# A written-out step order, eight plain products and accumulating transfers in the third stage and MLP of a spectral block

## The chip, the cores and the metric

The kernel runs on one core of a Trainium2 chip, in one launch. The metric is the device time of an execution in microseconds, as the median of several executions. The engines are TensorE (PE in the profile, with its weight loads as PEld), VectorE (DVE), ScalarE (ACT), GpSimd (POOL) and SyncE (SP). Each works off its own queue in order; they meet in semaphores. Transfers are issued from SP, ACT or GpSimd queues.

## The reference

```python
mod = (silu(c) @ w_mod).reshape(1, 6, 1, 512)
sa, ca, ga, sb, cb, gb = ...                # six vectors of 512
h = layernorm(x) * (1 + ca) + sa            # x: 2048 positions x 512
X = rfft2(h) * (w_r + 1j * w_i)
x = x + ga * irfft2(X, s=(2048, 512))
h = layernorm(x) * (1 + cb) + sb
h = h @ w1 + b1                             # 512 -> 1376
act = h * tanh(softplus(h))                 # Mish
x = x + gb * (act @ w2)                     # 1376 -> 512
```

All inputs and outputs are 32-bit floats.

## The kernel before, in words

`x` stays in on-chip memory as sixteen tiles `x[:, n, :]` of 128 positions by 512. The transforms are matrix products. The first stage takes rows and part of the columns forward, the second multiplies by the weights, and the third goes back: `p3_col(n)` does columns (16 short PE records at L744 and L745), ScalarE copies the result, `p3_row(n)` does rows (8 at L754) and VectorE adds them to `x` at L757. `norm_sums`, `norm_scale` and `norm_one` make the second layernorm of a tile; `transpose_in` and `scale_in` turn it so that features lie on partitions.

The MLP works on four pairs `i` of position blocks; a block `b` has 256 positions. The inputs of a pair are four quarters `B11`, `B21`, `B12`, `B22` (halves of the 512 features by block). The 1376 hidden features come in groups `t`: `t` = 1 to 5 have 256 each, `t` = 0 has the last 96. Matrix products use a reduced 32-bit format, so every operand is split in a high and a low part: ScalarE rounds to the high part, another engine subtracts for the low one (`split`, L791 and L792; `split_in`, L735 and L736; `split_w1`, L690 and L692), and three products (`TERMS`) are added for each.

For `t` > 0 both matrix products are made in seven products for eight, with sums of operand quarters. Going up, `up(i, t, j)` (L845) is product `j` of six matmuls of 256 columns; its operands are sums of w1 quarters (`sum_w1`, GpSimd at L686) and sums of inputs (`sum_in`, GpSimd at L731). `evict` takes the results out of the banks by ScalarE (L850, L868) and by additions on VectorE (L862, L866, L873); Mish is applied on ScalarE. The seven w1 operands of each `t` are written to DRAM once (`keep_w1`) and fetched for later pairs (`fetch_w1`, eight buffers `wr`).

Going down, `sums(b, t)` builds four 128-column sums on VectorE (L910), `halves` splits them into `ah` and `al`, and `down(b, t, c)` (L940, L936) is one of seven pieces of three matmuls; the w2 sums come from `sum_w2` (GpSimd at L788). After the last group `gather` copies two banks, `chain` adds on VectorE (L970 to L978), and `residual` applies the gate `gb` and adds to `x`, on GpSimd at L984 to L990. `store` writes two tiles of `x` to the output from SP. For the last block, `t` = 3, 4, 5 and 0 go down plainly with w2 rows that are already multiplied by the gate (`gate_w2`, GpSimd at L811), and `finish` adds and stores piece by piece.

The order of the work is that of a list: `plan.at(key, fn, ...)` notes a step with a number, `plan.run()` sorts by it and calls the steps, and each call appends its instructions to the queues of the engines. There are two such lists: one for the third stage with the weights' first preparation, and one for the MLP. In the first list, `plan_w1` prepares w1 groups 2, 3 and 1. In the second, every product has a place in `units`, and the others' keys are counted from these places.

Of the kernel before, what the change touches and what calls it, by code (L numbers as in the profile page):

```python
# [12 lines left out]
P = 128  # L13
# [6 lines left out]
NT = 6  # L20
# [8 lines left out]
FL = F - (NF - 1) * P  # L29
LAST = ((0, 0, D), (1, 0, D // 2), (1, D // 2, D))  # L30
POOL_LOW = range(1, 15, 2)


@with_exitstack
def tile_spectral_block(ctx: ExitStack, tc: tile.TileContext, x_d, w1_d, b1_d, w2_d,
# [615 lines left out]
    slots = {b: pm.tile([P, 2, 2, 256], F32R, name=f"h{b}", tag=f"h{b}") for b in ("B11", "B21", "T1", "T2", "T3", "T4")}  # L651
    wsum = pm.tile([P, 512], F32, name="wsum")
    ring, raws, src = {}, {}, {}
    near = ((1, "A11"), (2, "A11"), (1, "A12"), (1, "S2"), (1, "S1"), (1, "S3"), (2, "A12"), (1, "A22"))
# [4 lines left out]
    def load_w1(t, at, halves=range(2)):  # L659
        for i in halves:  # L660
            r = odd[at + i]
            nc.sync.dma_start(r.rearrange("p (k f) -> p k f", k=2), w1v[:, 2 * i:2 * i + 2, 256 * t - 256:256 * t])
            for j in range(2):
                src[t, f"A{j + 1}{i + 1}"] = r.rearrange("p (k f) -> p k f", k=2)[:, :, P * j:P * j + P]

    def space(t, a, k):
        if (t, a) in ring:
            return
        w = act.tile([P, 7, P], F32R, name=("ah", "al")[k % 2]).rearrange("p e s -> p (e s)")
        ring[t, a] = w[:, 0:512].rearrange("p (i k f) -> p i k f", i=2, k=2)  # L670
# [8 lines left out]
    def sum_w1(t, a):  # L679
        p, q, op = {"S1": ("A21", "A22", ALU.add), "S2": ("S1", "A11", ALU.subtract),  # L680
                    "S3": ("A11", "A21", ALU.subtract), "S4": ("A12", "S2", ALU.subtract)}[a]
        k = ("S1", "S2", "S4", "S3").index(a)
        if (t, a) in ((2, "S4"), (4, "S4"), (5, "S3")):
            src["S"] = even[2] if t < 4 else flat2(kiv) if t == 4 else buf("h")
        src[t, a] = (wsum if k < 2 else src["S"])[:, 256 * (k % 2):256 * (k % 2) + 256].rearrange("p (k f) -> p k f", k=2)
        nc.gpsimd.tensor_tensor(src[t, a], src[t, p], src[t, q], op=op)  # L686

    def split_w1(t, a):
        w = ring[t, a]
        nc.scalar.copy(w[:, 0], src[t, a])  # L690
        eng = nc.vector if a[0] == "A" else nc.gpsimd
        eng.tensor_tensor(w[:, 1], src[t, a], plain(w[:, 0]), op=ALU.subtract)  # L692

    def keep_w1(t, a):
        w = ring[t, a] if t > 3 or t == 1 and (t, a) in near else ring.pop((t, a))
        nc.sync.dma_start(kept[t, a], plain(w.rearrange("p i k f -> p (i k f)")))

    def single_w1(load):
        if load:
            src[0] = buf("g2")[:, 0:4 * FL].rearrange("p (k f) -> p k f", k=4)  # L700
            nc.sync.dma_start(src[0], w1v[:, :, (NF - 1) * P:F])
            return
        nc.scalar.copy(w1s[:, 0], src[0])
        nc.gpsimd.tensor_tensor(w1s[:, 1], src[0], plain(w1s[:, 0]), op=ALU.subtract)
# [22 lines left out]
    def sum_in(b, dst=None):  # L727
        p, q = {"T1": ("B12", "B11"), "T2": ("B22", "T1"), "T3": ("B22", "B12"), "T4": ("B21", "T2")}[b]
        p, q = raws[p], raws[q]
        raws[b] = raws[dst] if dst in raws else dst if dst is not None else buf("h")  # L730
        nc.gpsimd.tensor_tensor(raws[b], p, q, op=ALU.subtract)  # L731

    def split_in(b):
        r = raws[b]
        nc.scalar.copy(part(b, 0), r)  # L735
        nc.vector.tensor_tensor(part(b, 1), r, plain(part(b, 0)), op=ALU.subtract)  # L736
# [100 lines left out]

    def up(i, t, j):
        a, b = PRODUCTS[j]
        w, h = ring.pop((t, a)), slots[b]  # L840
        o = region(i, t, j)
        n = 0
        for p, q in TERMS:
            for k in range(2):
                nc.tensor.matmul(o, w[:, p, k, :], h[:, q, k, :], start=(j in (1, 5) and n == 0), stop=(n == 5),  # L845
                                 skip_group_check=True)
                n += 1

# [118 lines left out]
    def chain(b):  # L967
# [5 lines left out]
        if b == NB - 1:  # L973
            nc.vector.tensor_tensor(r0[:, 0:256], out_ps[b][2][:, 0:256], q[:, 256:], op=ALU.add)
            nc.gpsimd.tensor_tensor(r0[:, 256:], q[:, 256:], p[:, 256:], op=ALU.add)
# [5 lines left out]
    def residual(b):  # L981
        p, q = done.pop(b)
        r0, r1 = rows(b)
        nc.gpsimd.tensor_tensor(r1[:, 256:], r1[:, 256:], q[:, 0:256], op=ALU.add)  # L984
        if b < NB - 1:
            nc.gpsimd.tensor_tensor(r0[:, 256:], r0[:, 256:], p[:, 256:], op=ALU.add)
        for i, r in enumerate((r0, r1)):
            xb = x[:, 2 * b + i, :]
            nc.gpsimd.tensor_tensor(r, r, gbr, op=ALU.mult)
            nc.gpsimd.tensor_tensor(xb, xb, r, op=ALU.add)  # L990
# [16 lines left out]
    class Plan(list):  # L1007
# [7 lines left out]
    def plan_w1(plan, t, load, key, step, at):  # L1015
        k = 7 * (t - 2)
        plan.at(load, load_w1, t, at)
        for i, a in enumerate(("A11", "S1", "A12", "S2", "A22", "S4", "S3")):
            now = key + step * i
            plan.at(now, space, t, a, k + i)  # L1020
            if a[0] == "S":
                plan.at(now + 0.01, sum_w1, t, a)
            late = now + 0.02 if a[0] == "A" else now + 3.4 * step
            plan.at(late, split_w1, t, a)
            plan.at(late + 0.55 * step, keep_w1, t, a)

    plan = Plan()
    for s in range(N2 + 1):
        if s < N2:
            plan.at(s, p3_col, s)  # L1030
        if s:
            plan.at(s + 0.1, p3_row, s - 1)
            plan.at(s + 0.3, norm_sums, s - 1)
# [7 lines left out]
    for k, s in enumerate((0, 0, 1, 2, 3)):  # L1041
        plan.at(s + 0.05, late_mod, k)
    plan.at(5.08, plus_one, cols[:, 1, 1, :], cols[:, 1, 1, :])
    for lo, hi, s in ((0, 2, 4), (2, 4, 7), (4, 8, 13), (8, 12, 15)):
        plan.at(s + 0.2, norm_scale, lo, hi)
    for t, *at in ((1, 0, 2, 2, 3, 5), (2, 4, 8, 6, 7, 9), (3, 9, 11, 11, 12, 14)):
        for s, fn, *args in zip(at, (load_w2, split_w2, sum_w2, sum_w2, split_w2), (t,) * 5,
                                (None, False, 0, 2, True), (None, None, 1, 3, None)):
            plan.at(s + 0.6, fn, *[a for a in args if a is not None])
    plan.at(13.6, load_w2, 0)  # L1050
    plan.at(8.5, w2_space, 2)
    plan.at(16.5, w2_space, 4)
    plan.at(1.8, single_w1, True)
    plan.at(5.4, single_w1, False)
    plan_w1(plan, 2, 0.7, 2.1, 0.5, 0)
    plan_w1(plan, 3, 2.5, 5.7, 0.5, 2)
    for t, a in near:
        if t == 1:
            plan.at(9, slot_w1, (t, a))
        else:  # L1060
            plan.at(9, fetch_w1, t, a)
    plan_w1(plan, 1, 6.5, 9.3, 0.5, 0)
    plan.at(12, load_w1, 4, 2)
    first_raw = {}

    def first_in(b, n, g):
        first_raw[b] = buf("g2") if b in ("B11", "B21") else even[1 if b == "B12" else 0]
        transpose_in(n, g)
        scale_in(b, g, first_raw[b])

    for n, s in ((0, 5), (1, 6), (2, 8), (3, 9)):
        plan.at(s + 0.7, norm_one, n)
    for b, n, g, s in (("B11", 0, 0, 7), ("B21", 0, 1, 8), ("B12", 2, 0, 10), ("B22", 2, 1, 11)):
        plan.at(s + 0.55, first_in, b, n, g)
    for b, s, dst in (("T1", 12, "B11"), ("T2", 12, None), ("T3", 13, None), ("T4", 13, "B21")):
        plan.at(s + 0.5, sum_in, b, dst)
    for b, s in (("B11", 11), ("B21", 12), ("T2", 14), ("T1", 14.5), ("T3", 15), ("T4", 16)):
        plan.at(s + 0.4, split_in, b)
    plan.run()

    cr = big.tile([P, 2, 2, 2, 256], F32R, name="hcr", tag="cr")
    slots["B12"], slots["B22"] = cr[:, 0], cr[:, 1]
    odd[:] = [buf("g1"), buf("g1")] + odd
    turn = turns([even[2], odd[3], even[1], even[0], scb], [even[2], even[1], even[0], scb]), turns([], odd)

    units = [(0, 1, 1), (0, 2, 1), (0, 1, 2), (0, 1, 6), (0, 1, 5), (0, 1, 7), (0, 2, 2), (0, 1, 4), (0, 1, 3),
             (0, 2, 6), (0, 2, 5), (0, 2, 7)]
    for i in range(NB // 2):
        for t in range(1 if i else 3, NT):
            if t == NT - 1:  # L1090
                units += [(i, 0, u) for u in range(4)]
            prev = (i, t - 1) if t > 1 else (i - 1, NT - 1)
            units += [(i, t, 1)] + [prev + (j,) for j in (4, 3)] + [(i, t, j) for j in (6, 2, 5, 7)]
    units += [(NB // 2 - 1, NT - 1, j) for j in (4, 3)]
    where = {u: k for k, u in enumerate(units)}

    plan = Plan()
    for k, (i, t, j) in enumerate(units):
# [5 lines left out]
        plan.at(k, up, i, t, j)  # L1104
        plan.at(k + 0.05, evict, i, t, j)
        if j == 3:
            plan.at(k + 1.5, mish_odd, i, t)
        a = PRODUCTS[j][0]
        if i == 0 and t > 3:
            plan.at(k - 7.9, slot_w1, (t, a))  # L1110
            plan.at(k - (7.5 if t == 4 else 4.7), split_w1, t, a)
            plan.at(k - 3, keep_w1, t, a)
        elif k >= 8:
            plan.at(k - 7.9, fetch_w1, t, a)
    DOWN = (1, 2, 3, 0, 4, 5)
    start = {}
    key = where[0, 0, 0] + 0.25
    for b in range(NB):
        for t in DOWN if b < NB - 1 else (1, 2, 3, 4, 5, 0):
            if b == 0:  # L1120
                key = 0.25 + dict(zip(DOWN, (11, 18, 25, 32, 36, 42)))[t]
# [19 lines left out]
        plan.at(at + 1.6, residual, b)  # L1141
# [213 lines left out]
```

## Time and profile before

| | |
|---|---|
| median of 3 executions | 441.46 us (441.35 to 441.88) |
| the profiled execution | 443.01 us |
| its span, first to last instruction | 441.0 us |
| mean granted TensorE clock | 0.949 |
| busy: PE, DVE, ACT, POOL | 392.6, 333.1, 255.9, 203.1 us |

The span is the time between the first and the last instruction that the profile shows. A group's row gives line, engine, operation, out<-in tiles with shapes, count, then busy microseconds, mean nanoseconds of one, and idle time of the engine before it with what ended it. In a row of waits stand the waiting engine and what it was to write, the one waited for, microseconds in total, times, and the longest. In a row of a time window stand its bounds and length, busy time and count for each engine, the granted clock, and the transfers' share and rate. In a timeline row stand start and duration in microseconds; pieces of the chain of work that ended last have the same two numbers in front.

### The profile page before, as it was taken

The page shows a single profiled execution, that of the slowest core. Times are in us where ns is not written, and L with a number is a line of the kernel's source. Part 1 is how long each engine was busy: PE and PEld are TensorE (multiplying, and loading weights), DVE is VectorE, ACT ScalarE, POOL GpSimd, SP SyncE. Part 2 cuts the span into 40 slices and gives each one's busy share as a digit, 9 for nine tenths or more (in the row PEclk, how much of TensorE's full clock was granted, in tenths as well). Part 3 has the DMA queues.
Part 4 walks back from the last instruction along what each step waited for, and adds up shares of the span by engine and source line. Part 5 has one row for each costly group of instructions (what it writes and reads, how often), then busy time and mean ns, then how long its engine had stood idle before and what let it go on. Part 6 is the DMA issues. An engine that isn't in the chain of part 4 may idle for free.

```text
span 441.0 us, 8229 instructions
## 1 busy us (share of the span) xinstructions
PE 392.6 (89%) x2886; PEld 368.3 (84%) x2886; DVE 333.1 (76%) x659; ACT 255.9 (58%) x560; POOL 203.1 (46%) x227
## 2 busy tenths in 40 slices
PE   9999999999897667996979998979998979999576
PEld 8899777799897667986869998969998969998465
DVE  2999778869899676646783599783599894599984
ACT  2888799845784268853627746526746623535430
POOL 0687488826779034273050075050075060086554
PEclk9999999999998878996989999988999999999969
DMA  8999987766583667174636526535527546624011
GB/s 265 366 350 329 358 287 241 239 210 216 187 281 111 207 214 217 47 255 150 191 107 203 169 76 211 171 107 184 167 89 217 158 115 205 187 78 138 24 49 48
DMA packets 45593, 81.87 MB, mean 186 GB/s; under 512 B 6992, under 2 KB 12208, under 8 KB 45296
## 3 DMA queue, kind: packets, MB, share of 16 engines
q1 hardware_dynamic: 43392, 74.39, 52.3%
q10 hardware_dynamic: 2160, 6.95, 5.0%
q8 instruction: 23, 0.38, 0.4%
q14 instruction: 18, 0.15, 0.1%
HBM read 67.95 MB, written 13.37 MB: 184 GB/s over the span
## 4 chain that ended last, share of the span: by engine, by line
PE 50%; DVE 33%; ACT 7%; DMA 4%; issue 4%; POOL 1%; SPq 1%; DVEq 0%; ACTq 0%; POOLq 0%
PE bank L845 14%; PE bank L940 11%; DVE buf L910 10%; DVE al L792 7%; PE bank L500 3%; PE bank L210 3%; PE bank L549 2%; PE bank L255 2%; DVE w2a L792 2%; PE bank L480 2%; DVE hB L736 2%; DMA w_S<-al 2%; DVE st L124 1%; ACT ah L791 1%; PE bank L952 1%
## 5 line engine op out<-in xcount | busy, mean ns | idle before, releaser
L845 PE MATMUL bank<-hT,wr 128*128 128x256 f32 x480 | 76.3, 299 | 15.5 <-DVE even L862 8.7
L845 PEld LDWEIGHTS bank<-hT,wr 128*128 128x128 f32 x480 | 67.8, 206 | 17.2 <-DVE even L862 9.5
L984 POOL TENSOR_TENSOR modr<-modr,buf 128x256 f32<-128x256 f32 x7 | 6.6, 942 | 126.9 <-DVE buf L971 126.9
L791 ACT CAST ah<-buf 128x512 fp32r<-128x512 f32 (+1 forms) x45 | 27.0, 603 | 42.0 <-DVE buf L910 38.4
L792 DVE TENSOR_TENSOR al<-buf,ah 128x512 fp32r<-128x512 f32 (+1 forms) x45 | 42.8, 957 | 8.9 <-ACT ah L791 8.5
L845 PE MATMUL bank<-hB,wr 128*128 128x256 f32 x240 | 40.8, 313 | 1.8 <-ACT odd L850 1.7
L940 PE MATMUL bank<-w2a,ah 128*128 128x256 f32 x161 | 39.5, 309 | 0.0
L845 PEld LDWEIGHTS bank<-hB,wr 128*128 128x128 f32 x240 | 35.6, 216 | 3.6 <-ACT odd L850 2.9
L940 PE MATMUL bank<-w2b,ah 128*128 128x256 f32 x147 | 33.8, 291 | 0.0
L940 PEld LDWEIGHTS bank<-w2a,ah 128*128 128x128 f32 x161 | 30.5, 219 | 0.0
L940 PE MATMUL bank<-w2a,al 128*128 128x256 f32 x56 | 18.8, 336 | 10.8 <-DVE al L792 10.8
L850 ACT ACTIVATE odd<-bank,b1n 128x256 f32<-128x256 f32 x25 | 11.8, 474 | 27.4 <-PE bank L845 27.3
L940 PEld LDWEIGHTS bank<-w2b,ah 128*128 128x128 f32 x147 | 25.6, 199 | 0.0
L744 PE MATMUL bank<-kc,d 128*128 128x128 f32 x128 | 24.8, 276 | 0.5 <-ACT d L393 0.5
L745 PE MATMUL bank<-kc,d 128*128 128x128 f32 x128 | 24.8, 275 | 0.0
L940 PE MATMUL bank<-w,ah 128*128 128x256 f32 x112 | 22.9, 296 | 0.6 <-DVE modr L978 0.5
L940 PEld LDWEIGHTS bank<-w2a,al 128*128 128x128 f32 x56 | 12.9, 231 | 12.6 <-DVE al L792 12.6
L731 POOL TENSOR_TENSOR buf<-buf 128x512 f32<-128x512 f32 x13 | 18.2, 1411 | 9.5 <-DVE hB L736 8.1
L124 DVE BATCH_NORM_STATS2 st<-x 128x6 f32<-128x512 f32 x32 | 22.0, 688 | 0.3
L990 POOL TENSOR_TENSOR x<-x,modr 128x512 f32<-128x512 f32 x14 | 21.0, 1501 | 1.1
L754 PE MATMUL bank<-kiv,buf 128*128 128x128 f32 x128 | 18.1, 287 | 3.5 <-DVE x L757 2.7
L255 PE MATMUL bank<-buf,mring 128*128 128x512 f32 x48 | 20.6, 430 | 0.2 <-DVE buf L248 0.2
(308 smaller groups left out, 1261.4 us busy)
## 6 DMA issues: line engine op xcount, KB each, us to landing
wr<-w_S SPq DMA_DIRECT2D x69, 256.0 KB, 2.8
wr<-w_A SPq DMA_DIRECT2D x51, 256.0 KB, 2.8
x<-in_A_x_dram SPq DMA_DIRECT2D x16, 256.0 KB, 5.1
xring<-in_x_t_dram SPq DMA_DIRECT2D x16, 256.0 KB, 5.1
out_dram<-x SPq DMA_DIRECT2D x7, 512.0 KB, 4.0
buf<-in_B_w_dram SPq DMA_DIRECT2D x12, 256.0 KB, 3.9
w_S<-wr SPq DMA_DIRECT2D x11, 256.0 KB, 3.0
odd<-in_B_w_dram SPq DMA_DIRECT2D x10, 256.0 KB, 3.4
```

The lines of the kernel that those rows point to most:

```text
L124: nc.vector.bn_stats(t, x[:, n, :])
L255: nc.tensor.matmul(pa, m[:, a, 0:128], g, start=(i == 0), stop=False)
L731: nc.gpsimd.tensor_tensor(raws[b], p, q, op=ALU.subtract)
L744: nc.tensor.matmul(o, dj[:, 0:128], kc[0][:, n, :], start=True, stop=False)
L745: nc.tensor.matmul(o, dj[:, 64:192], kc[1][:, n, :], start=False, stop=True)
L754: nc.tensor.matmul(px[:, j * P:(j + 1) * P], e[:, j * P:(j + 1) * P], kiv[:, j, :], start=True, stop=True)
L791: nc.scalar.copy(h, r)
L792: nc.vector.tensor_tensor(l, r, plain(h), op=ALU.subtract)
L845: nc.tensor.matmul(o, w[:, p, k, :], h[:, q, k, :], start=(j in (1, 5) and n == 0), stop=(n == 5), skip_group_check=True)
L910: nc.vector.tensor_tensor(o, p, q, op=op)
L940: nc.tensor.matmul(out_ps[b][n][:, 256 * half:256 * half + 256], a[p][:, e], w2[t][q][:, r], start=(t == 1 and half == 0 and i == 0), stop ...
L990: nc.gpsimd.tensor_tensor(xb, xb, r, op=ALU.add)
```

## The change

The third stage and the MLP become one list of 1155 steps. Its keys are sorted as before, and then the steps are called in the order that the string `ORDER` writes out by place in the sorted list.

The first pair of blocks (512 positions) is computed with eight plain products for `t` = 1 to 5: each quarter of the result is accumulated in a bank and evicted by one Mish activation on ScalarE (`plain_evict`). Its w1 quarters are split into the buffers from which `up` reads them (`block_w1`), three of the four are kept for later pairs.

The four sums of w1 quarters, which only later pairs read, are built in place by transfers from DRAM that add to their destination, issued from the GpSimd queue (`sum_w1`, steps 0 and 1); step 2 splits a sum and writes it out. The residual of blocks 0 to 6 is multiplied by the gate in one VectorE instruction of 1024 columns and added to `x` by such a transfer. All other arithmetic that GpSimd did in these stages goes to VectorE.

```diff
--- before.py
+++ after.py
...
+PLAIN = {(0, t) for t in range(1, NT)}
...
+ORDER = (
+    "3-4 71 0-1 16 21 2 15 14 5-7 73 38 47 8 12 9 62 13 10 69 86 17 24 84 52 19 79 11 26 126 95 18 22 32 23 87 27 "
...
+    def load_w1(t):
+        src[t] = shared("T1" if t % 2 else "T2").rearrange("p (k f) -> p k f", k=4)
+        nc.sync.dma_start(src[t], w1v[:, :, 256 * t - 256:256 * t])
 
...
+    def split_w1(w, r):
+        nc.scalar.copy(w[:, 0], r)
+        nc.vector.tensor_tensor(w[:, 1], r, plain(w[:, 0]), op=ALU.subtract)
+
+    def block_w1(t, a):
+        slot_w1((t, a))
+        split_w1(ring[t, a], w1_block(t, a, src[t]))
+
+    def keep_w1(t, a, w=None):
+        w = ring[t, a] if w is None else w
         nc.sync.dma_start(kept[t, a], plain(w.rearrange("p i k f -> p (i k f)")))
+
+    def sum_w1(t, a, step):
+        if not temps:
+            temps[0] = shared("T4").rearrange("p (n k f) -> p n k f", n=4, k=2)
+            temps[1] = wsum.rearrange("p (n k f) -> p n k f", n=2, k=2)
+            stage[0] = shared("T3", F32R).rearrange("p (n i k f) -> p n i k f", n=2, i=2, k=2)
+        v = temps[1][:, a == "S3"] if t % 3 == 0 else temps[0][:, 2 * (t % 3 - 1) + (a == "S3")]
+        if step == 0:
+            if a == "S3":
+                nc.scalar.mul(v, w1_block(t, "A21", src[t]), -1.0)
+            if a == "S2":
+                nc.scalar.mul(v, v, -1.0)
+            if a == "S1":
+                nc.sync.dma_start(v, w1_block(t, "A21"))
+                return
+        if step < 2:
+            nc.gpsimd.dma_start(v, w1_block(t, {"S1": "A22", "S2": "A11", "S3": "A11", "S4": "A12"}[a]), accum_op=ALU.add)
+            return
+        n = stage[1] = stage.get(1, 0) + 1
+        w = stage[0][:, n % 2]
+        split_w1(w, v)
+        keep_w1(t, a, w)
 
...
-        p, q = {"T1": ("B12", "B11"), "T2": ("B22", "T1"), "T3": ("B22", "B12"), "T4": ("B21", "T2")}[b]
+        p, q, op = {"T1": ("B12", "B11", ALU.subtract), "T2": ("T1", "B22", ALU.subtract),
+                    "T3": ("B22", "B12", ALU.subtract), "T4": ("B21", "T2", ALU.add)}[b]
         p, q = raws[p], raws[q]
         raws[b] = raws[dst] if dst in raws else dst if dst is not None else buf("h")
-        nc.gpsimd.tensor_tensor(raws[b], p, q, op=ALU.subtract)
+        nc.vector.tensor_tensor(raws[b], p, q, op=op)
...
-            nc.gpsimd.tensor_tensor(tsum[:, o], a, b, op=ALU.subtract)
+            nc.vector.tensor_tensor(tsum[:, o], a, b, op=ALU.subtract)
...
-            nc.gpsimd.tensor_tensor(r, r, gbr[:r.shape[0]], op=ALU.mult)
+            nc.vector.tensor_tensor(r, r, gbr[:r.shape[0]], op=ALU.mult)
...
+    def plain_place(t, f, e):
+        return (e, f) if t == 1 else (f, e)
+
     def up(i, t, j):
-        a, b = PRODUCTS[j]
-        w, h = ring.pop((t, a)), slots[b]
-        o = region(i, t, j)
+        a, b = j if (i, t) in PLAIN else PRODUCTS[j]
+        w, h = ring[t, a], slots[b]
+        if (i, t) in PLAIN:
+            at, half = plain_place(t, int(a[1]) - 1, int(b[2]) - 1)
+            if (i, t, at) not in ups:
+                ups[i, t, at] = bank("AD"[at])
+            o = ups[i, t, at][:, 256 * half:256 * half + 256]
+            first, last = a[2] == "1" and half == 0, a[2] == "2"
+        else:
+            o = region(i, t, j)
+            first, last = j in (1, 5), True
         n = 0
         for p, q in TERMS:
             for k in range(2):
-                nc.tensor.matmul(o, w[:, p, k, :], h[:, q, k, :], start=(j in (1, 5) and n == 0), stop=(n == 5),
+                nc.tensor.matmul(o, w[:, p, k, :], h[:, q, k, :], start=(first and n == 0), stop=(last and n == 5),
                                  skip_group_check=True)
                 n += 1
+
+    def plain_evict(i, t, f, e):
+        b = 2 * i + e
+        if (b, t) not in raw:
+            hold(b, t)
+        at, half = plain_place(t, f, e)
+        nc.scalar.activation(raw[b, t][:, 256 * f:256 * f + 256], ups[i, t, at][:, 256 * half:256 * half + 256], AF.Mish,
+                             bias=b1n[:, 2 * t - 2 + f:2 * t - 1 + f])
 
...
-    def residual(b):
-        p, q = done.pop(b)
+    def residual(b, step):
+        p, q = done[b]
         r0, r1 = rows(b)
-        nc.gpsimd.tensor_tensor(r1[:, 256:], r1[:, 256:], q[:, 0:256], op=ALU.add)
+        if step == 0:
+            nc.vector.tensor_tensor(r1[:, 256:], r1[:, 256:], q[:, 0:256], op=ALU.add)
+            if b < NB - 1:
+                nc.vector.tensor_tensor(r0[:, 256:], r0[:, 256:], p[:, 256:], op=ALU.add)
+            return
         if b < NB - 1:
-            nc.gpsimd.tensor_tensor(r0[:, 256:], r0[:, 256:], p[:, 256:], op=ALU.add)
+            r = modr[:, 0:2]
+            nc.vector.tensor_tensor(r, r, gbr.unsqueeze(1).to_broadcast([P, 2, D]), op=ALU.mult)
+            nc.gpsimd.dma_start(x[:, 2 * b:2 * b + 2, :], r, accum_op=ALU.add)
+            return
         for i, r in enumerate((r0, r1)):
             xb = x[:, 2 * b + i, :]
-            nc.gpsimd.tensor_tensor(r, r, gbr, op=ALU.mult)
-            nc.gpsimd.tensor_tensor(xb, xb, r, op=ALU.add)
+            nc.vector.tensor_tensor(r, r, gbr, op=ALU.mult)
+            nc.vector.tensor_tensor(xb, xb, r, op=ALU.add)
 
...
-            for _, _, fn, args in sorted(self, key=lambda e: e[:2]):
+            steps = [e[2:] for e in sorted(self, key=lambda e: e[:2])]
+            places = [[int(n) for n in run.split("-")] for run in ORDER.split()]
+            places = [k for run in places for k in range(run[0], run[-1] + 1)]
+            assert sorted(places) == list(range(len(steps)))
+            for k in places:
+                fn, args = steps[k]
                 fn(*args)
...
+    S_KEYS = ((1, -5, 1 / 3), (2, 4, 1.7), (3, 11, 1.5), (4, 18, 1.4), (5, 26, 1.1))
     plan = Plan()
...
+    for n in range(N2):
+        last = n == N2 - 1
+        plan.at(n - N2, p3_col, n)
+        plan.at(1.5 if last else n - N2 + 1.1, p3_row, n)
+        plan.at(1.6 if last else n - N2 + 1.3, norm_sums, n)
 
...
+    for t, key in ((1, -15.3), (2, -13.5), (3, -3.9), (4, 5), (5, 12.6)):
+        plan.at(key, load_w1, t)
...
+    for t, key, scale in S_KEYS:
+        for a, step, at in (("S1", 0, 0), ("S3", 0, 0.5), ("S1", 1, 2.2), ("S3", 2, 4), ("S1", 2, 5.5), ("S2", 0, 5.9),
+                            ("S2", 2, 9), ("S4", 1, 9.6), ("S4", 2, 12.6)):
+            plan.at(key + scale * at, sum_w1, t, a, step)
+
...
             plan.at(k, up_single, i, j)
@@ -1102,23 +1206,23 @@
                 plan.at(k + 0.05, evict_single, i)
             continue
         plan.at(k, up, i, t, j)
+        if (i, t) in PLAIN:
+            f, e = int(j[0][1]) - 1, int(j[1][2]) - 1
+            at, half = plain_place(t, f, e)
+            if j[0][2] == "2" and half:
+                for h in range(2):
+                    plan.at(k + 0.05, plain_evict, i, t, *((h, e) if t == 1 else (f, h)))
+            continue
         plan.at(k + 0.05, evict, i, t, j)
         if j == 3:
             plan.at(k + 1.5, mish_odd, i, t)
...
+        plan.at(k - 7.9, fetch_w1, t, PRODUCTS[j][0])
...
-        plan.at(at + 1.6, residual, b)
+        plan.at(at + 1.6, residual, b, 0)
+        plan.at(at + 2.6, residual, b, 1)
         plan.at(at + 9, store, b)
...
```

More of the change, by code (lines that the diff above doesn't have):

```diff
@@ L1079, in tile_spectral_block, with late_slots @@
[L1079 to L1087, printed above, removed]
+        plan.at(s - N2 + 0.55, first_in, b, n, g)
+    def late_slots():
+        cr = big.tile([P, 2, 2, 2, 256], F32R, name="hcr", tag="cr")
+        slots["B12"], slots["B22"] = cr[:, 0], cr[:, 1]
```

197 lines of the change are left out of this document (78 added, 119 removed), and 43 rows, old and new, of the table ORDER.

## The prediction, made blind

> **What bounds the kernel now.** I read the page's totals first, then the busy times of three stretches, then what TensorE waits for, and last the timeline around one of these waits.
>
> ```profile
> span 441.0 us, 8229 instructions
> ...
> PE 392.6 (89%) x2886; PEld 368.3 (84%) x2886; DVE 333.1 (76%) x659; ACT 255.9 (58%) x560; POOL 203.1 (46%) x227
> ```
>
> No engine is full over the span, so the stage has to be found. The change begins where the third stage does (first row below, 90.2 us). I cut there, at the first product of the second pair of position blocks (204.60) and of the fourth (336.91).
>
> ```profile
> 90.22 0.49 PE L744 MATMUL bank<-kc,d 128*128 128x128 f32 x2 [0.46 <-ACT d L393]
> ...
> 204.60 0.84 PE L845 MATMUL bank<-hB,wr 128*128 128x256 f32 x3
> ...
> 336.91 0.76 PE L845 MATMUL bank<-hB,wr 128*128 128x256 f32 x5
> ```
>
> ```profile
> core 0: us, PE busy (x) PEld busy (x) DVE busy (x) ACT busy (x) POOL busy (x), PEclk, DMA share, GB/s
> 90.20:204.60 114.40, 94.58 (x719) 91.45 (x720) 87.72 (x168) 70.04 (x156) 61.64 (x69) 0.91 0.59 194
> 204.60:336.90 132.30, 123.17 (x954) 120.51 (x954) 92.86 (x179) 72.39 (x151) 40.06 (x32) 0.95 0.51 152
> 336.90:441.00 104.10, 87.43 (x638) 82.32 (x636) 80.63 (x139) 42.50 (x88) 42.78 (x33) 0.95 0.38 120
> ```
>
> A busy PE isn't a PE at its peak, so I price its work by the chain's undisturbed pieces, the third being the same work at half clock:
>
> ```profile
> 94.06 0.89 PE bank L754 x8
> ...
> 233.77 0.72 PE bank L940 x6
> ...
> 163.33 1.28 PE bank L940 x6
> ```
>
> A short (128-column) record is 0.111 us, a 256-column matmul 0.12, a 512-column one twice that. Counted over the listing, the first stretch holds 416 short records (384 of the third stage, 32 transposes) and 303 matmuls: 46.3 + 36.4 = 82.7 us of 114.4. The second holds 32 and 921: 114.1 of 132.3. The third holds 615 and 21 wide ones: 78.8 of 104.1. So 31.7, 18.2 and 25.3 us are lost there. The granted clock accounts for part (0.09 x 114.4 = 10.3; 0.05 x 132.3 = 6.6; 5.2), the last transfer for 2.7 (the last addition starts at 437.91), and waits for the rest: 21.4, 11.6 and 17.4 us.
>
> ```profile
> 437.91 0.42 DVE L1002 TENSOR_TENSOR x<-x,bank 128x256 f32<-128x256 f32 x1 [0.58 <-PE bank L955]
> ```
>
> What TensorE waits for is VectorE, in the whole run (first three rows) and at 142 to 205 us (last two):
>
> ```profile
> PE bank L940 <- DVE al L792: 16.5, 13, 3.7
> PE bank L845 <- DVE even L862: 8.7, 4, 3.5
> PE bank L845 <- DVE scb L862: 5.4, 2, 4.2
> ...
> PE bank L845 <- DVE even L862: 6.2, 2, 3.5
> PE bank L845 <- DVE scb L862: 4.2, 1, 4.2
> ```
>
> VectorE is late although it has idle time, and the timeline shows why. While GpSimd applies the residual, four 128-column sums take 3.59 us; four others, 7 us later and without GpSimd, 1.01. Two subtractions take 3.30.
>
> ```profile
> 286.99 3.59 DVE L910 TENSOR_TENSOR buf<-buf 128x128 f32<-128x128 f32 x4
> 287.64 1.29 POOL L989 TENSOR_TENSOR modr<-modr 128x512 f32<-128x512 f32 x1
> 289.01 1.41 POOL L990 TENSOR_TENSOR x<-x,modr 128x512 f32<-128x512 f32 x1
> 290.39 1.31 POOL L989 TENSOR_TENSOR modr<-modr 128x512 f32<-128x512 f32 x1
> 290.50 3.30 DVE L792 TENSOR_TENSOR al<-buf,ah 128x384 fp32r<-128x384 f32 x2
> 291.78 1.47 POOL L990 TENSOR_TENSOR x<-x,modr 128x512 f32<-128x512 f32 x1
> 292.17 0.39 PE L940 MATMUL bank<-w2a,al 128*128 128x256 f32 x1 [1.97 <-DVE al L792]
> 294.06 1.01 DVE L910 TENSOR_TENSOR buf<-buf 128x128 f32<-128x128 f32 x4
> 294.19 1.65 PE L845 MATMUL bank<-hT,wr 128*128 128x256 f32 x6 [1.27 <-DVE even L862]
> ```
>
> TensorE stands for 1.97 and 1.27 us, and its next six matmuls take 1.65 instead of 0.72: each wait is paid again in clock.
>
> **The change, part by part.** VectorE, undisturbed, by width (minimum/median/maximum in ns):
>
> ```profile
> L792 DVE TENSOR_TENSOR al<-buf,ah x45: 552/692/1779, 160.7 to 430.6; 128x512 fp32r<-128x512 f32 x39, 128x384 fp32r<-128x384 f32 x6
> L792 DVE TENSOR_TENSOR w<-modr,w x1: 1207/1207/1207, 110.1 to 110.1; 128x1024 fp32r<-128x1024 f32 x1
> L862 DVE TENSOR_TENSOR even<-even,bank x15: 405/415/421, 148.0 to 397.6; 128x256 f32<-128x256 f32 x15
> L910 DVE TENSOR_TENSOR buf<-even x30: 276/284/1396, 157.6 to 406.5; 128x128 f32<-128x128 f32 x30
> L124 DVE BATCH_NORM_STATS2 st<-x 128x6 f32<-128x512 f32 x32 | 22.0, 688 | 0.3
> L125 DVE BATCH_NORM_AGGREGATE mv<-st 128x2 f32<-128x6 f32 x32 | 5.8, 182 | 1.1
> ```
>
> So 1024 columns cost 1.21 us, 512 0.69, 384 0.55, 256 0.42, 128 0.28, statistics 0.87, the smallest ones 0.16 by estimate. At these prices the listing of before gives 77.0, 80.7 and 59.2 us, 216.9 in all; 87.72 + 92.86 + 80.63 = 261.2 were taken. About 44 us of VectorE's time is waiting for GpSimd's arithmetic.
>
> *GpSimd's arithmetic goes (144.5 us in the three stretches), VectorE takes most of it.* Added there: 20 w2 sums and 20 low halves of w1 sums of 256 columns, one of 384 (8.4 + 8.4 + 0.6); 12 input sums of 512 (8.3; the first pair has none any more); in the residual 16 of 256, 7 of 1024, 4 of 512 (6.7 + 8.5 + 2.8); 7 gatings of 512 (4.8); 5 low halves of A21 (2.1). Taken away with the first pair's seven products: 15 additions of 256 and 4 splits of 512 (6.3 + 2.8). Net +41.5. So VectorE's load is 258.4 where 261.2 was measured: 85.0, 94.6 and 78.8 by stretch. The gain is not a lighter VectorE. It is that an instruction which TensorE waits for takes 0.28 or 0.69 us instead of up to 1.4 or 1.8, and that the moved 41.5 us can be queued where nothing waits. What stands behind them in VectorE's queue are the sums and splits of the next step; in the new order the residual's 1.21 us multiplication stands 11 to 46 steps behind its additions, in the second stretch behind sums and splits of two later groups.
>
> *First 512 positions plain.* Eight products of six matmuls for seven, five times: 30 x 0.12 = +3.6 us on TensorE, in the first stretch (315 matmuls, 84.1 us) and the third, as the new order moves work on: 915 (113.4) and 639 plus 21 wide (81.7). In exchange no product of the first pair waits for an addition to `even` or `scb`, the two rows of 6.2 and 4.2 us, and ScalarE alone evicts. The extra 3.6 us are on the path, as TensorE is.
>
> *w1 sums by accumulating transfers.* 20 of 128 KB and, for the residual, 7 of 512 KB. No row shows an accumulating transfer. Plain neighbours:
>
> ```profile
> w_A<-wr SPq DMA_DIRECT2D x9, 256.0 KB, 2.4
> out_dram<-x SPq DMA_DIRECT2D x7, 512.0 KB, 4.0
> wm<-in_w_mod_dram SPq DMA_DIRECT2D x7, 256.0 KB, 9.4
> ```
>
> From below 2.4 us, from above the 9.4 of a loaded queue; I take 5, as the destination is read as well, near the first row doubled. The new order leaves, in priced load, 4 to 7 us between issue and consumer for 10 of the 20 and 8 to 25 for the others; at the pace forecast some 15% more. At 5 us next to nothing is late (under 1 us in all). At 8 us the ten would be late by 18 in sum; that is in the range. The Trainium skill's page DMA: Bandwidth & Descriptors (Anatomy of one DMA) fits a transfer issued by GpSimd as 2.0 us plus bytes over 436 GB/s, an estimate of 2.3 us for 128 KB, by which the sum would be the same. The residual's seven are read only by the stores, 10 us of work later, but the last one's store stands on SP ahead of the last output.
>
> *Written-out order and one plan.* The third stage and the first products share one list: VectorE has 48 us of priced work before the first product, which came 51.7 us after the stage's start:
>
> ```profile
> L845 PE MATMUL bank<-hB,wr x240: 277/283/561, 141.9 to 397.1; 128*128 128x256 f32 x120
> ```
>
> So the third stage itself gains little.
>
> **The sum.** The clock's loss is taken to shrink with the waits. First stretch: 84.1 of work; waits 21.4 less the two rows' 10.4, that is 11.0; clock 10.3 to 5.3: 100.4. Second: 113.4; waits 11.6 less two block boundaries of 1.97 + 1.27, 5.1; clock 6.6 to 2.9: 121.4. Third: 81.7; VectorE and TensorE are nearly equal here, so I let only 10 of 17.4 us of waits go; 7.4, clock 5.2 to 2.2, last transfer 2.7: 94.0. Together 315.8 for 350.8, 35.0 less: 406.0 of span. The profiled execution took 443.01 for its 441.0, 2.0 around it, and lies 1.55 above the median 441.46; from the median the forecast is 406.5.
>
> **Rivals.** *The waits nearly vanish.* Half of what I leave in waits and clock goes too (11.0 + 5.3 + 5.1 + 2.9 + 7.4 + 2.2 = 33.9 us): 17 less, 389.5. For it: undisturbed VectorE is ahead almost everywhere in the second stretch (94.6 against 113.4).
>
> *VectorE becomes the bound* where it has TensorE's load: 85.0 against 84.1 in the first stretch, 78.8 against 81.7 in the third. Then the waits that I let go there, 10.4 and 10, come back on VectorE, with little of the clock, as TensorE's pauses are short: 406.5 + 20 = 426 at worst, and 422 with some of them gone. Against it: VectorE had 87.72 of 114.40 and 80.63 of 104.10.
>
> *Slower: accumulating transfers land late.* VectorE and ScalarE stop in order at the split of a sum, in the stretch with no slack, so what is late is paid by all. From 8 us (18 late) each further us costs ten more, and the wait is paid again in clock: at 12 us 58 us late, 406 + 58 = 464 at worst, about 455 with some overlap. It decides from about 10 us, just over the slowest row (9.4). Against it: the sums are issued from a queue that holds nothing else. The Trainium skill's page SBUF — State Buffer (SBUF: two separate sides) says that such transfers starve while VectorE runs an instruction that takes both ports, copies above all; none of VectorE's additions and subtractions here is a copy, and no run here shows it.
>
> *The order does nothing:* all waits stay, and 30 products are added: 441.5 + 3.6 = 445.
>
> **How the numbers follow.** Forecast 0.47, waits vanish 0.13, VectorE bound 0.24: faster 0.84. Late transfers 0.10, order without effect 0.04: slower 0.14, within 0.2% (what a measurement of this kernel can tell from no change, 0.9 us) 0.02. The range runs from 387, a little under the better rival, to 436, over the VectorE rival plus most of the 18 us of 8-us transfers; beyond it lie the slower cases, 0.16.
>
> **What would show it.** Right: no GpSimd arithmetic after 90 us; VectorE near 258 us in the three stretches, and no sum of 128 columns over 0.4 us; waits of TensorE on VectorE under 20 us; granted clock 0.95 or more in the first stretch. Wrong: ScalarE or VectorE waiting for DMA at the splits of w1 sums; VectorE over 95% busy in the first stretch; or TensorE waiting as long as before, on other lines.

## The result and the profile after

The changed kernel takes 411.57 us (median, 409.60 to 412.34), the kernel before 441.67 beside it (441.35 to 442.62). The ratio is 0.9308, 95% interval 0.9272 to 0.9345. The forecast was 406.5. The profiled execution took 411.89 us for a span of 409.7, so the three stretches can be set against the forecast one by one.

First the page's totals after, and the head of its chain of work that ended last (shares of the span). The second fence is the chain's row before:

```profile
span 409.7 us, 8223 instructions
...
PE 378.2 (92%) x2916; PEld 358.9 (88%) x2916; DVE 299.5 (73%) x732; ACT 254.8 (62%) x563; POOL 89.4 (22%) x122
...
PE 41%; DVE 4%; DMA 3%; ACT 3%; issue 2%; DVEq 0%; ACTq 0%
```

```profile
PE 50%; DVE 33%; ACT 7%; DMA 4%; issue 4%; POOL 1%; SPq 1%; DVEq 0%; ACTq 0%; POOLq 0%
```

VectorE has 4 of the 53% that the chain after adds up to, where it had 33 of 100. This chain is followed back only to 187 us, though, so it says nothing of the first stretch. GpSimd's busy time is less than half of what it was. The busy times of the stretches, cut at the same instructions as before (first product of the third stage, of the second pair, of the fourth):

```profile
core 0: us, PE busy (x) PEld busy (x) DVE busy (x) ACT busy (x) POOL busy (x), PEclk, DMA share, GB/s
91.30:199.80 108.50, 90.52 (x731) 88.44 (x732) 75.20 (x188) 67.48 (x153) 23.21 (x19) 0.94 0.66 176
199.80:320.50 120.70, 117.91 (x947) 116.72 (x948) 82.75 (x206) 73.25 (x155) 5.09 (x5) 0.97 0.67 189
320.50:409.70 89.20, 82.76 (x662) 80.70 (x660) 69.96 (x164) 42.97 (x90) 3.45 (x4) 0.99 0.59 173
```

Forecast were 100.4, 121.4 and 94.0. The total is near (318.4 for 315.8), but the first stretch is 8.1 too long and the third 4.8 too short. The waits in the first stretch say what the first is waiting for:

```profile
DVE hT L727 <- ACT hT L726: 19.3, 8, 6.8
...
ACT hT L726 <- DMA hT<-in_B_w_dram: 13.1, 4, 6.7
...
ACT hT L726 <- DMA wsum<-in_B_w_dram: 6.8, 1, 6.8
PE bank L818 <- ACT buf L811: 5.7, 1, 5.7
PE bank L920 <- ACT buf L929: 5.2, 1, 5.2
```

L726 is ScalarE's half of a split of a w1 sum. It stands 19.9 us for accumulating transfers. VectorE, which subtracts at L727, stands behind it, and so does TensorE, which needs copies and activations queued behind that split (L811, L929). Its waits on VectorE, over 30 us in the three largest rows before, are nearly gone. These are all of 0.5 us and more, in the three stretches together:

```profile
PE bank L1023 <- DVE al L856: 1.5, 2, 0.9
PE bank L818 <- DVE x L821: 1.5, 2, 1.3
PE bank L920 <- DVE scb L945: 0.7, 1, 0.7
```

Why the sums are late is seen in GpSimd's timeline (start, duration, what it issues, idle time before it and what ended that):

```profile
102.39 1.23 POOL L752 DMA_DIRECT2D hT<-in_B_w_dram  x1 [4.19 <-issue]
106.34 1.21 POOL L752 DMA_DIRECT2D hT<-in_B_w_dram  x1 [2.73 <-issue]
111.66 1.22 POOL L752 DMA_DIRECT2D hT<-in_B_w_dram  x1 [4.11 <-issue]
...
126.06 1.21 POOL L752 DMA_DIRECT2D wsum<-in_B_w_dram  x1 [5.38 <-issue]
131.26 1.21 POOL L752 DMA_DIRECT2D wsum<-in_B_w_dram  x1 [3.98 <-ACT w2hi L855]
135.16 1.22 POOL L752 DMA_DIRECT2D hT<-in_B_w_dram  x1 [2.70 <-issue]
```

"issue" means that the profile shows nothing that GpSimd waited for. The landings in the trace do: the transfer issued at 102.39 landed at 106.08 and the next started at 106.34; that one landed at 111.34, next 111.66; 131.26 landed at 134.85, next 135.16. In 14 of the 19 cases the next starts some 0.3 us after the landing. In all 19 the transfer before has landed: there is one of these transfers under way at a time.

### The profile page after: what moved, and what is told of

The parts are those of the page before. It is cut to its first block, busy times and chain, and to the rows that moved or that the text cites. A ratio compares the mean times of both kernels' runs of the same rounds, so it can differ in the third digit from the quotient of the medians.

```text
span 409.7 us, 8223 instructions
## 1 busy us (share of the span) xinstructions
PE 378.2 (92%) x2916; PEld 358.9 (88%) x2916; DVE 299.5 (73%) x732; ACT 254.8 (62%) x563; POOL 89.4 (22%) x122
## 4 chain that ended last, share of the span: by engine, by line
PE 41%; DVE 4%; DMA 3%; ACT 3%; issue 2%; DVEq 0%; ACTq 0%
PE bank L1023 19%; PE bank L920 17%; PE bank L969 2%; PE bank L1019 2%; DMA buf<-in_B_w_dram 1%; DMA hT<-in_B_w_dram 1%; ACT ah L855 1%; DVE al L856 1%; PE bank L774 1%; DMA wr<-w_A 1%; PE bank L1035 1%; DVE buf L993 1%; DVE x L1080 0%; DVE hT L800 0%; ACT hcr L799 0%
## 5 line engine op out<-in xcount | busy, mean ns | idle before, releaser
L920 PE MATMUL bank<-hB,wr 128*128 128x256 f32 x300 | 46.9, 297 | 9.6 <-ACT buf L929 5.2
L920 PE MATMUL bank<-hT,wr 128*128 128x256 f32 x360 | 52.2, 285 | 1.1 <-DVE scb L945 0.7
L920 PEld LDWEIGHTS bank<-hB,wr 128*128 128x128 f32 x300 | 41.4, 202 | 10.7 <-ACT buf L929 5.4
L920 PEld LDWEIGHTS bank<-hT,wr 128*128 128x128 f32 x360 | 47.0, 192 | 1.6 <-DVE scb L945 0.9
L752 POOL DMA_DIRECT2D hT<-in_B_w_dram x16 | 19.7, 1230 | 72.6 <-issue 26.0
L856 DVE TENSOR_TENSOR al<-buf,ah 128x512 fp32r<-128x512 f32 (+1 forms) x45 | 30.0, 670 | 5.3 <-ACT ah L855 4.8
L920 PE MATMUL bank<-hcr,wr 128*128 128x256 f32 x210 | 30.7, 285 | 0.0
L920 PEld LDWEIGHTS bank<-hcr,wr 128*128 128x128 f32 x210 | 27.7, 194 | 0.1
L726 ACT CAST hT<-hT 128x256 fp32r<-128x256 f32 x16 | 6.5, 404 | 30.0 <-DMA hT<-in_B_w_dram 20.7
L818 PEld LDWEIGHTS bank<-kiv,buf 128*128 128x128 f32 x128 | 16.3, 200 | 8.3 <-ACT buf L811 6.5
L727 DVE TENSOR_TENSOR hT<-hT,hT 128x256 fp32r<-128x256 f32 x16 | 6.8, 424 | 20.7 <-ACT hT L726 20.7
```

The source lines that it names most:

```text
L727: nc.vector.tensor_tensor(w[:, 1], r, plain(w[:, 0]), op=ALU.subtract)
L752: nc.gpsimd.dma_start(v, w1_block(t, {"S1": "A22", "S2": "A11", "S3": "A11", "S4": "A12"}[a]), accum_op=ALU.add)
L818: nc.tensor.matmul(px[:, j * P:(j + 1) * P], e[:, j * P:(j + 1) * P], kiv[:, j, :], start=True, stop=True)
L856: nc.vector.tensor_tensor(l, r, plain(h), op=ALU.subtract)
L920: nc.tensor.matmul(o, w[:, p, k, :], h[:, q, k, :], start=(first and n == 0), stop=(last and n == 5), skip_group_check=True)
```

## Experiments

All times are medians beside the kernel before, which took 441.7 to 444.7 us in the sets of runs; the ratio is to that.

**More room for descriptors.** The descriptors of a GpSimd transfer (the entries that say what to move where) lie in rings in a reserved piece of on-chip memory, whose size the program sets, in bytes per partition. (The Trainium skill's page DMA: Bandwidth & Descriptors, section SWDGE vs HWDGE vs iDMA, says that the rings live in such a piece; how many transfers it holds it doesn't say.)

```diff
-    nc = _bacc.Bacc(..., dynamic_dma_scratch_size=1024)
+    nc = _bacc.Bacc(..., dynamic_dma_scratch_size=1664)
```

> The changed kernel with 1664 instead of 1024 bytes per partition for the descriptors of transfers issued by GpSimd, and nothing else. In the changed kernel 14 of the 20 w1 accumulating transfers are issued 0.3 us after the one before has landed, so only one is in flight, and ScalarE waits for them 20 us in the first stretch. Theory (room for descriptors holds them back): issues come closer than 2 us where their data are ready, ScalarE's wait for them falls from 20 to under 10 us, and the time falls by 4 to 8 us, to 404 to 408. Rival (each transfer waits for the one before for another reason, such as a semaphore or an order kept by the queue): the same spacing and 411.5 within 1.5 us.

Measured: 389.75 us (386.44 to 391.81), ratio 0.8777 (0.8737 to 0.8817): the direction is right, the size is about three to five times the expected (21.8 us for 4 to 8). Its stretches and GpSimd's timeline:

```profile
90.16:180.45 90.29, 85.56 (x731) 84.52 (x732) 74.41 (x188) 68.05 (x153) 24.37 (x20) 1.00 0.80 212
180.45:298.21 117.76, 116.56 (x947) 115.33 (x948) 82.67 (x206) 73.31 (x155) 3.84 (x4) 0.99 0.68 193
298.21:387.50 89.29, 82.73 (x662) 80.66 (x660) 69.97 (x164) 43.01 (x90) 3.42 (x4) 0.99 0.60 173
```

```profile
117.20 1.20 POOL L752 DMA_DIRECT2D hT<-in_B_w_dram  x1 [6.47 <-DVE hT L727]
117.93 1.70 POOL L752 DMA_DIRECT2D wsum<-in_B_w_dram  x1
121.47 1.22 POOL L752 DMA_DIRECT2D wsum<-in_B_w_dram  x1 [1.83 <-ACT wsum L745]
```

The first two landed at 123.42 and 125.64, so three are under way at 121.5, and what GpSimd waits for is now mostly the work before a transfer: its idle time marked "issue" falls from 37.7 to 1.1 us. Of the 22 us, 18.2 are from the first stretch, whose clock rises from 0.94 to 1.00.

**Without the sums' transfers.** This takes all their cost away; the later pairs then multiply by unfinished sums.

```diff
-            nc.gpsimd.dma_start(v, w1_block(...), accum_op=ALU.add)
             return
```

> Leaves out the 20 accumulating transfers of the w1 sums, so later pairs multiply by unfinished sums; splits and all else stay in place. Theory (late sums are what the first stretch lost against the forecast): TensorE's waits behind ScalarE of 5.7 and 5.2 us go with some of the clock, the first stretch falls from 108.5 to 98 to 101 us, and the time to 402 to 405. Rival (VectorE bounds the first stretch): the stretch stays over 105 and the time over 408.

Measured: 380.19 us (379.50 to 380.50), ratio 0.8576 (0.8550 to 0.8602), over 20 us below what was expected.

```profile
90.52:175.07 84.55, 84.53 (x731) 84.37 (x732) 73.75 (x187) 67.69 (x154) 1.16 (x1) 1.00 0.60 195
175.07:289.84 114.77, 114.30 (x950) 113.53 (x948) 83.41 (x208) 73.28 (x155) 2.78 (x3) 1.00 0.67 199
289.84:378.10 88.26, 82.59 (x662) 80.66 (x660) 70.05 (x164) 43.01 (x90) 3.45 (x4) 0.99 0.59 175
```

TensorE is busy all through the first two stretches, at full clock. The transfers cost 31.4 us altogether (411.57 less 380.19), 21.8 of which go with the larger room.

**Room in smaller steps.**

```diff
-    nc = _bacc.Bacc(..., dynamic_dma_scratch_size=1024)
+    nc = _bacc.Bacc(..., dynamic_dma_scratch_size=1152)
...
+    nc = _bacc.Bacc(..., dynamic_dma_scratch_size=1280)
```

> Descriptor room 1152 B instead of 1024, nothing else. A transfer of a w1 sum has 272 packets, 17 for each of 16 engines; one is under way with 1024 B, two with 1664 B. Theory (a transfer is issued when the room for all of its descriptors is free, so the room counts in whole transfers): either still one under way and 408 to 414 us, or already two and 387 to 393 us, nothing between. Rival (the room is filled piece by piece): the next issue starts somewhat sooner, and the time is between, 395 to 407.

> Descriptor room 1280 B, nothing else. As before: by whole transfers 387 to 393 us with two under way, or 408 to 414 with one; by pieces between, 390 to 400.

One execution each: 390.62 and 389.47 us. Whole transfers it is: 128 B more give all of the gain. With 1152 B two are under way, and the third of the same group waits for a landing (the one issued at 117.03 landed at 123.65):

```profile
117.03 1.21 POOL L752 DMA_DIRECT2D hT<-in_B_w_dram  x1 [6.79 <-DVE hT L727]
117.77 1.71 POOL L752 DMA_DIRECT2D wsum<-in_B_w_dram  x1
123.97 1.22 POOL L752 DMA_DIRECT2D wsum<-in_B_w_dram  x1 [4.48 <-issue]
```

So one fits in 1024 B, two in 1152 and three in 1664: by these counts one takes over 512 B (half of 1024) and at most 555 B (a third of 1664). The "two with 1664 B" in the expectation was a misreading.

**The same transfers as plain copies, room 1024 B.** Is it the queue, or the adding?

```diff
-            nc.gpsimd.dma_start(v, w1_block(...), accum_op=ALU.add)
+            nc.gpsimd.dma_start(v, w1_block(...))
```

> The changed kernel with the 20 transfers of the w1 sums as plain copies from the same queue: same bytes, same places, nothing added to the destination (the output isn't the reference's). Theory: the cost lies in the queue, which has one transfer under way at a time with the room of 1024 B, and not in the adding: 405 to 414 us, landing 3.5 us or more. Rival: adding at the destination makes a transfer slow: landing near 2.5 us and 385 to 398 us.

Measured: 386.98 us (384.12 to 388.20), ratio 0.8729 (0.8684 to 0.8773). The theory falls, and the rival's reason too. The time from issue to landing is nearly the same (minimum/median/maximum, the changed kernel first, then this one):

```profile
DMA to landing us min/median/max: 3.5/4.6/7.7
```

```profile
DMA to landing us min/median/max: 2.7/4.6/6.9
```

What differs is the number of packets in GpSimd's queue (packets, MB, share of the transfer engines' time; the same order):

```profile
q0 software_dynamic: 6448, 6.29, 10.8%
```

```profile
q0 software_dynamic: 1968, 6.29, 8.6%
```

Without the sums 1008 are left, so a sum of 128 KB takes 272 packets when it adds and 48 as a copy. Copies overlap at 1024 B: those issued at 117.44 and 118.16 landed at 123.46 and 124.53. So it is neither the queue alone nor the adding alone: adding makes six times the packets, and 272 fill the room. That packets are what fills it is argued from these counts; no run varied the packets of an accumulating transfer.

**Later splits.** Room 1664 B, and besides splits of sums moved back in the order.

```diff
-    "... 24 84 52 19 79 11 26 126 95 18 22 32 23 87 27 37 ... 97 49 43 111 99 93 ..."
+    "... 24 52 19 79 11 26 126 95 18 22 32 23 84 27 37 ... 93 171 50 61 119 57 53 97 99 ..."
```

> Descriptor room 1664 B as in the 389.75 us run, and besides eight splits of w1 sums that stood 1.4 to 7 us behind their transfer moved back in the written-out order to 5 to 8 us behind it, with the steps that need their buffers. Theory: the 9.6 us that separate 389.75 from the 380.2 without these transfers are late sums: 383 to 387. Rival: they are the traffic and the order of the rest: 388.5 to 391.

Measured: 392.33 us (389.12 to 394.38), ratio 0.8857 (0.8815 to 0.8900): no gain over 389.75. ScalarE's wait for sums in the first stretch fell from 5.5 us to 0.6, yet the stretch took 92.8 us for 90.3. But ScalarE now stands 3.3 us for the write-out of an earlier sum and 1.5 us for w2 rows, so the move took one wait away and brought others. What the last 9.6 us are stays open. Plain copies of the same bytes already cost 6.8 (386.98 less 380.19).

**The order alone.** The steps in the order of their keys, everything else as changed.

```diff
-ORDER = ("3-4 71 0-1 16 21 ... 1154 1153 ")
+ORDER = "0-1154"
```

> The changed kernel with its steps in the order of their keys, without the written-out permutation. Theory (the gain comes from GpSimd's arithmetic being off VectorE's path, the permutation only trims): 412 to 425. Rival (the written-out order carries the gain): 430 or more, with TensorE's waits for VectorE back over 25 us.

Measured: 455.93 us (453.82 to 458.04), ratio 1.0287 (1.0244 to 1.0329). All but the order makes the kernel slower than before. The theory falls. The rival's time came, but not its waits: from 90 us on TensorE waits 12.4 us on VectorE, not over 25, and 41.4 on ScalarE. The stretches (TensorE's counts show that other work lies between the cuts here: 776 records for 731):

```profile
90.20:236.00 145.80, 105.89 (x776) 101.64 (x777) 77.94 (x194) 71.68 (x159) 24.55 (x20) 0.85 0.55 146
236.00:356.40 120.40, 115.47 (x919) 113.88 (x918) 84.22 (x203) 73.35 (x152) 3.52 (x4) 0.96 0.65 186
356.40:453.90 97.50, 85.71 (x647) 81.98 (x645) 68.33 (x161) 42.47 (x88) 2.59 (x3) 0.96 0.50 145
```

```profile
ACT hT L681 <- DMA hT<-in_B_w_dram: 34.8, 11, 5.0
...
ACT hT L681 <- DMA wsum<-in_B_w_dram: 13.8, 3, 5.7
```

ScalarE waits 48.6 us for sums in the first stretch, so order and sums had to be told apart.

**The order of the keys, larger room.**

```diff
-ORDER = ("3-4 71 ...")
+ORDER = "0-1154"
...
-    nc = _bacc.Bacc(..., dynamic_dma_scratch_size=1024)
+    nc = _bacc.Bacc(..., dynamic_dma_scratch_size=1664)
```

> The steps in the order of their keys, as in the 455.9 us run, but with the descriptor room of 1664 B, which let two accumulating transfers be under way. Theory A: most of what the order of the keys costs is late sums of w1 (ScalarE waited 30 us for them in the first stretch, 19 in the second): 455.9 falls by 35 to 55 us, to 400 to 420. Theory B: the order places VectorE's and ScalarE's work badly by itself, and the sums only show it: 430 or more. The stretch from the first product of the second pair on should be near 215 us by both, as it is (120.4 + 97.5) without the larger room.

Measured: 429.53 us (427.53 to 430.59), ratio 0.9696 (0.9644 to 0.9747). The fall of 26.4 us is less than theory A asked for, and the time lies just under theory B's. From the second pair on it takes 218.2 us, as said.

**The order of the keys, no sums' transfers.**

```diff
-ORDER = ("3-4 71 ...")
+ORDER = "0-1154"
...
-            nc.gpsimd.dma_start(v, w1_block(...), accum_op=ALU.add)
             return
```

> The steps in the order of their keys and without the 20 accumulating transfers of the w1 sums (the output isn't the reference's). What is left over the 380.2 us of the written-out order without these transfers is the price of the order of the keys by itself. Theory A (the order matters through the late sums): 380 to 395. Theory B (it matters by itself): 405 or more.

Measured: 411.23 us (409.94 to 413.64), ratio 0.9292 (0.9247 to 0.9337). Theory B holds. In one table, medians in us:

| | room 1024 B | room 1664 B | no transfers of sums |
|---|---|---|---|
| written-out order | 411.57 | 389.75 | 380.19 |
| order of the keys | 455.93 | 429.53 | 411.23 |
| difference | 44.4 | 39.8 | 31.0 |

The order is worth 31 us by itself, and 13 more at 1024 B as it spares part of the late sums. Without the transfers TensorE still waits 21.7 us in the keys' order (on ScalarE and VectorE, from 90 us on) and 1.8 in the written-out one.

**The residual back on GpSimd's arithmetic** (blocks 0 to 6).

```diff
-            nc.vector.tensor_tensor(r1[:, 256:], ...)
+            eng = nc.gpsimd if b < NB - 1 else nc.vector
+            eng.tensor_tensor(r1[:, 256:], ...)
             if b < NB - 1:
-                nc.vector.tensor_tensor(r0[:, 256:], ...)
+                nc.gpsimd.tensor_tensor(r0[:, 256:], ...)
...
-            nc.vector.tensor_tensor(r, r, gbr..., op=ALU.mult)
-            nc.gpsimd.dma_start(x[:, 2 * b:2 * b + 2, :], r, accum_op=ALU.add)
+            for i, r in enumerate((r0, r1)):
+                xb = x[:, 2 * b + i, :]
+                nc.gpsimd.tensor_tensor(r, r, gbr, op=ALU.mult)
+                nc.gpsimd.tensor_tensor(xb, xb, r, op=ALU.add)
```

> The changed kernel with the residual of blocks 0 to 6 back on GpSimd: additions, gate and addition to x as before, no accumulating transfer to x. Theory (GpSimd's arithmetic lengthens VectorE's instructions where TensorE waits): sums of 128 columns reach over 1 us again, the second stretch grows from 120.7 by 5 to 9 us, the third by 2 to 6, and the time is 418 to 426. Rival (the order alone removed the waits, and VectorE gains 2 us per block by losing the residual's work): 407 to 413.

Measured: 432.09 us (428.80 to 433.28), ratio 0.9737 (0.9694 to 0.9780): 20.5 more than the changed kernel, beyond the range expected. Sums queued behind arithmetic could have done that, so it was repeated with the larger room.

> Descriptor room 1664 B, so that late sums cost little, and the residual of blocks 0 to 6 back on GpSimd's arithmetic. Theory (GpSimd's arithmetic makes VectorE's instructions slow and TensorE waits for them, whatever the sums do): about 20 us over the 389.75 of the same room, as at 1024 B (432.1 against 411.6): 405 to 414, nearly all after the first product of the second pair. Rival (the 20 us came from a GpSimd queue in which sums waited behind arithmetic): 390 to 396.

Measured: 411.27 us (410.12 to 412.89), ratio 0.9284 (0.9216 to 0.9352): 21.5 over the same room without this arithmetic.

```profile
89.53:179.56 90.03, 85.64 (x732) 84.52 (x732) 74.41 (x188) 68.44 (x154) 24.45 (x20) 1.00 0.80 213
179.56:308.43 128.87, 118.12 (x947) 115.54 (x948) 94.98 (x196) 73.28 (x155) 32.19 (x25) 0.99 0.56 169
308.43:409.40 100.97, 88.89 (x661) 85.37 (x660) 76.72 (x153) 42.99 (x90) 23.50 (x18) 0.94 0.40 127
```

Nothing changes before the first residual (90.0 for 90.3), then the stretches grow by 11.1 and 11.7 us. VectorE does 10 instructions fewer in the second and is busy 12.3 us longer. TensorE's waits on VectorE are back: 16.2 us after 179.5 us, where the same room without this arithmetic has 1.5. The two largest rows:

```profile
PE bank L920 <- DVE even L945: 5.8, 3, 2.8
...
PE bank L1023 <- DVE al L856: 4.6, 5, 1.4
```

A group of its 128-column sums, here and then in the changed kernel (busy time, mean ns of one):

```profile
L993 DVE TENSOR_TENSOR buf<-buf 128x128 f32<-128x128 f32 x24 | 10.6, 481 | 0.2
```

```profile
L993 DVE TENSOR_TENSOR buf<-buf 128x128 f32<-128x128 f32 x24 | 5.9, 286 | 0.2
```

The Trainium skill's page SBUF — State Buffer (Who interferes with whom) says that a VectorE instruction with two inputs in SBUF, the on-chip memory that holds `x`, contends with a GpSimd instruction that reads SBUF. These runs agree, with 481 against 286 ns.

## Why the prediction was right, point by point

**The total was right by two errors that cancel, and that is luck.** The work of TensorE was priced well: 84.1 and 113.4 us in the first two stretches, and without the sums' transfers they take 84.55 and 114.77. Beyond that two steps failed.

- *The clock and the waits left in.* I kept 11.0 + 5.3, 5.1 + 2.9 and 7.4 + 2.2 us of them. Without the transfers 0.5, 1.4 and, beside the last transfer of 2.7, 3.9 are left (88.26 less 81.7 and 2.7): 33.9 priced, 5.7 measured. That is the rival "the waits nearly vanish", which I gave 0.13. Its 389.5 us and the 389.75 of the larger room agree by chance: it let half of the 33.9 go; without the transfers nearly all of it is gone, and the larger room still pays 9.6 us for them.
- *"At 5 us next to nothing is late."* The flight of 5 us was a good guess (3.5/4.6/7.7), but I put the transfers beside one another. One at a time, a transfer starts when the last has landed, and lateness adds up along the queue. The transfers cost 24.0 us in the first stretch (108.50 less 84.55), 5.9 in the second and 0.9 in the third, against under 1 us priced; 21.8 us of time go with the larger room and are the price of one at a time, and for the other 9.6 no run shows the reason. The argument against the rival with late transfers, "a queue that holds nothing else", was the sentence that failed: an empty queue is no use if the next transfer can't be started. That rival's mechanism was there; it lost to the first error's gain, and so the sign held: the forecast 315.8, less 28.2 of waits and clock (33.9 less 5.7), plus 30.8 of transfers, is the 318.4 measured. In the order of the keys it wins: 44.7 us are lost to the sums there (455.93 less 411.23), and the change is slower than before.

**VectorE's load.** Forecast 258.4 us, shown busy 227.9 (75.20 + 82.75 + 69.96). The pricing itself was right: the durations of the 557 VectorE records add up to 259.3. But records of queued instructions overlap, 389 of them by 83 ns in the median. VectorE's timeline after shows it:

```profile
288.76 0.28 DVE L993 TENSOR_TENSOR buf<-odd 128x128 f32<-128x128 f32 x1
289.08 0.29 DVE L993 TENSOR_TENSOR buf<-buf,odd 128x128 f32<-128x128 f32 x1
289.29 0.28 DVE L993 TENSOR_TENSOR buf<-odd 128x128 f32<-128x128 f32 x1
289.49 0.29 DVE L993 TENSOR_TENSOR buf<-odd,buf 128x128 f32<-128x128 f32 x1
```

The last two start 0.21 and 0.20 us after the one before, which lasts 0.28 or 0.29. I set a sum of durations against a busy time, in which overlaps count once. So "the gain is not a lighter VectorE" was wrong: its busy time fell by 33.3 us (261.2 to 227.9), and the sum of its durations by 26 (from 285.6 before), with 41.5 us of work moved to it. The 44 us put down to GpSimd's arithmetic were too few by the same mistake: 285.6 less the 216.9 priced are 69. The rival "VectorE becomes the bound" never came near (69%, 69% and 78% busy). The row that would have warned me was in the prediction: four sums of 0.284 us in 1.01 us.

**GpSimd's arithmetic beside VectorE** was the right mechanism: the residual alone costs 20.5 and 21.5 us of time. With the larger room it adds 11.1 and 11.7 us to the second and third stretches, where the sum had let 10.2 and 13.0 of waits and clock go for all of GpSimd's arithmetic. The w2 sums, splits and input sums that moved too were not varied by themselves.

**First 512 positions plain.** 3.6 us of TensorE priced, and the page shows the 30 more records (2916 for 2886); the work in which they stand was met to 1.4 us in the first and second stretches without transfers. Not varied by itself.

**The order.** "The third stage itself gains little" held in the changed kernel for a reason that I did not have: the first product starts 53.8 us after the stage does (51.7 before), but 44.4 with the larger room, less than the 48 us of VectorE's work that I took to stand before it. So late sums hid a gain of 7 us there. "The order does nothing" falls by 31 to 44 us.

**The signs named.** No sum of 128 columns is over 0.4 us, and the waits on VectorE are under 20 us (3.7): as said. Of GpSimd's arithmetic one unchanged instruction is left after 90 us, L624 at 90.86. The clock of the first stretch, 0.94, just missed 0.95. One of the wrong-signs came true, ScalarE waiting for transfers at the splits, and it points to the step that failed.

## What to carry to other kernels

Before a chain of transfers from GpSimd is priced by its flight, ask how many can be under way: if a new issue follows each landing by 0.3 us and the profile calls the wait "issue", try more descriptor room first; here 128 B were worth 21 us of 411. Compare sums of record durations only with sums of durations, busy times only with busy times. And test an order and the transfers that it hides together: here each changed the other's worth by 13 us.

## What the runs showed of the hardware

- An accumulating transfer of 128 KB takes 272 packets, a plain one from the same queue 48, and GpSimd 1.21 us to issue instead of 0.72. The median flight is 4.6 us for both at 1024 B, and 5.8 for accumulating ones at 1664 B, where up to three are under way.
- The descriptor room counts in whole transfers: 1024 B hold one such transfer, 1152 two, 1664 three. One against two is 411.6 against 390.6 us; two (one execution at each of two sizes) against three makes no difference here.
- TensorE shows a granted clock of 1.00 in first stretches in which it is busy for 84.53 of 84.55 and 85.56 of 90.29 us, and 0.85 in the one with the most waits (145.8 us, order of the keys).
